# A Fourier convolution with a token-choice layer behind it: sums made in place and in other stages, and PSUM in two pools

## The chip, the cores and the metric

The kernel runs on one core of one Trainium2 chip. The metric is the device time of one execution in microseconds (us), lower is better.

## What is computed

The first part convolves every channel of `x` (8 batches, 6336 positions, 128 channels) with a filter `h` of the same length. The second part scores each position, picks the 128 best positions of each batch and adds a small gated two-layer network there.

```python
Xf = np.fft.rfft(x, n=2 * S, axis=1)
Hf = np.fft.rfft(h, n=2 * S, axis=0)
y = np.fft.irfft(Xf * Hf[None], n=2 * S, axis=1)[:, :S]
scores = np.einsum('bsd,d->bs', y, w_gate)
out = y.copy()
for b in range(B):
    top = np.argpartition(-scores[b], 128)[:128]
    ye = np.maximum(y[b, top] @ w1, 0) @ w2
    out[b, top] = y[b, top] + sigmoid(scores[b, top])[:, None] * ye
```

## The kernel before

The length 6336 is 99 x 64 (`N1` x `N2`), and the transform is done as matmuls in float32 over these two factors. Two batches at a time make a group, `g` = 0 to 3. The channels are taken in two halves of 64, `u` = 0 and 1. Each half of a group's `x` lies in one half of the tile `slots`, as eight blocks of 1024 columns, each with an upper part of 512 columns and a lower one. The stages of a group are generators, and `mix` (L481) interleaves them: at each step of its first argument it takes a given rate of steps of the others. The order of the instructions on each engine is this program order, since the schedule is manual (L40).

- **Stage A** (`stage_a`, L168) transforms over n1. For each block, `turn` (L158) makes on VectorE (DVE) the sum and the difference of the upper and the lower part, 114x512 each, into two tiles `xs` of the pool's tag "t", which has six buffers and also holds `tx` and `tm`. Eight blocks of two units: a unit is 16 matmuls into a tile of two PSUM banks, and one copy of 128x792 out of it, on ScalarE (ACT) or DVE. It turns at most three blocks ahead.
- **Stage b** (`stage_b`, L248, with `over_n2`, L228): 25 chunks of four frequencies. A chunk is 8 matmuls into the first bank of a tile `p`, two ACT operations that write the swapped and negated copy into its second bank (L234, L235), two DVE multiplications with the filter's spectrum (L239: into `slots`, and into `tx`), and an addition on GpSimd (POOL, L246). Tables `w` and spectra `hr` are loaded ahead on the SyncE queue (SP).
- **Stage c** (`stage_c`, L255): 16 units for each `u`, 16 matmuls into two banks and a copy of 99x1024.
- **Stage d** (`stage_d`, L265): 16 units of 8 matmuls, a copy, the store of the output and the scores (POOL multiplies, L287, DVE reduces, L289).
- **The choice** (`pick`, L292) of the group before runs beside all this as `side`, a chain on DVE with small matmuls: two searches of eight steps, then the places of the chosen rows (`lane`, written into `cmp`, L388 and L390), and a last matmul with them (L400). `feed` (L434) is the small network.

A group runs A for u=0, then b for u=0 with A for u=1 mixed in, then b for u=1 with c for u=0 (and `side`), then c for u=1 (with `side`), then d (with `side`). Group 0 has `stage_first` (L196), which also makes the filter's spectrum, in place of its first b. `stage_twice` (L222) copies half of that spectrum to a second place in memory; in group 0 it is mixed into c for u=1, and b for u=1 loads that half twice instead. The load of a group's second half of `x` starts when the d before it has ended, since its place is in use until then; the first half is loaded one stage earlier.

All PSUM tiles come from one pool of four tiles of two banks (L44), also those that use one bank.

Of the kernel before, what the change touches and what calls it, by code (L numbers as in the profile page):

```python
# [36 lines left out]
def conv_moe(ctx, tc, x, h, w_gate, w1, w2, fx_d, wb_d, wc_d, at_d, tri_d, cst_d, out):  # L37
# [6 lines left out]
    pp_ = ctx.enter_context(tc.tile_pool(name="pp_", bufs=4, space=PSUM))  # L44
# [5 lines left out]
    def bank():  # L50
        return banks()[:, 0:512]

    def psm():
        return pp_.tile([128, 1024], F32, tag="p", name="m")[:, 0:512]
# [56 lines left out]
    def ahead(key, only=None):  # L111
# [29 lines left out]
        while loaded[1] < len(spectra) and loaded[1] <= i + DEEP:  # L141
            item = spectra[loaded[1]]
            if item[1] != key[1]:
                break
            ht = hr[:, loaded[1] % 8 * 512:loaded[1] % 8 * 512 + 512].rearrange("p (t k d) -> p t k d", t=2, d=HD)
            loaded[1] += 1
            k0, kn = kchunks[item[3]]
            once = item[1:3] == (0, 1)
            for e in (slice(0, 64), slice(64, 128)) if once else (slice(0, 128),):
                nc.sync.dma_start(out=ht[e, :, 0:kn], in_=hd[0:64 if once else 128, item[2], item[3], :, 0:kn])  # L150
            have["h", item] = ht
# [4 lines left out]
    turned = {}  # L156

    def turn(d0):  # L158
# [9 lines left out]
    def stage_a(half, c0, lead=()):  # L168


        blocks = [(half, d) for d in range(0, HD, 8)]
        todo = blocks + list(lead)
        yv = yp[:, c0 // 2:(c0 + D) // 2].rearrange("p (b j) k t -> p b j t k", b=2)
        for i, d0 in enumerate(blocks):
            for d in todo[i:i + 3]:
# [20 lines left out]
    def stage_first():  # L196


        for ci, (k0, kn) in enumerate(kchunks):
# [19 lines left out]
            over_n2(0, k0, kn, wt, hv[:, 0])  # L219
            yield  # L220

    def stage_twice():  # L222

        for ci, (k0, kn) in enumerate(kchunks):
            nc.sync.dma_start(out=hd[64:128, 1, ci, :, 0:kn], in_=hd[0:64, 1, ci, :, 0:kn])
            yield

    def over_n2(c0, k0, kn, wt, ht, adds=nc.gpsimd):  # L228

        pt = banks()  # L230
        for j in range(kn):
            product(pt[:, j * D:(j + 1) * D], wt[:, j], row(k0 + j, c0, D))
        pv, pw = (pt[:, o:o + kn * D].rearrange("p (k b) -> p k b", b=D) for o in (0, 512))
# [4 lines left out]
        def times(dst, src, t):  # L238
            v.tensor_tensor(out=dst, in0=src.rearrange("p k (b j t) -> p k b j t", b=2, t=2),  # L239
# [8 lines left out]
    def stage_b(g, u, adds=(nc.gpsimd,)):  # L248
        for ci, (k0, kn) in enumerate(kchunks):
            key = ("b", g, u, ci)  # L250
            ahead(key)
            over_n2(u * D, k0, kn, have.pop(key), have.pop(("h", key)), adds[ci % len(adds)])
            yield

# [10 lines left out]
    def stage_d(g, ss):  # L265
# [3 lines left out]
        for m0 in range(0, N2, nd):  # L269
# [14 lines left out]
            for b in range(nb):  # L284
                tm = tp.tile([N1, nd, D], F32, tag="t", name="tm", bufs=6)
# [218 lines left out]
    rest(stage_a(0, D, [(1, 0), (1, 8)]))  # L504
# [3 lines left out]
    for i, _ in enumerate(stage_first()):  # L508
        if NK - 12 <= i < NK - 4:
            load(x[0, 1], 0, [i - NK + 12])  # L510
    ahead(("b", 0, 1, 0))
    side = iter(())
    twice = stage_twice()
    fed = []
    for g in range(G):
        last = g == G - 1
        c = stage_c(0, (1, 1, 0))
        if g:
            mix(stage_a(0, 0, [(1, 0), (1, 8)]), (side, 0.1))
            a = stage_a(1, D)  # L520
# [9 lines left out]
        mix(b, (c, 0.67 if g else 0.4), (side, 0.2))  # L530
# [9 lines left out]
        mix(stage_c(1, (1,)), (side, 0.9), (twice, 1.6))  # L540
# [9 lines left out]
        rest(twice)  # L550
# [96 lines left out]
```

## Time and profile before

| | |
|---|---|
| median of 3 runs | 1041.99 us (1041.69 to 1043.3) |
| the profiled execution, its own time | 1042.09 us |
| its span | 1040.3 us |
| TensorE (PE) busy | 909.1 us, 87% |
| DVE busy | 648.2 us, 62% |
| ACT busy | 554.5 us, 53% |
| POOL busy | 436.1 us, 42% |
| mean granted TensorE clock | 0.941 of 2.4 GHz |

The span runs from the first instruction to the last; the execution's own time is 1.8 us longer. PE is the busiest engine over the span, but the shares are means over stages that have different limits, so the stages have to be read one at a time. PE records come two to a float32 matmul: a unit of A or c is 32 records, a chunk of b 16.

### The profile page before, as it was taken

The page shows a single profiled execution, that of the slowest core. Times are in us where ns is not written, and L with a number is a line of the kernel's source. Part 1 is how long each engine was busy: PE and PEld are TensorE (multiplying, and loading weights), DVE is VectorE, ACT ScalarE, POOL GpSimd, SP SyncE. Part 2 cuts the span into 40 slices and gives each one's busy share as a digit, 9 for nine tenths or more (in the row PEclk, how much of TensorE's full clock was granted, in tenths as well). Part 3 has the DMA queues.
Part 4 walks back from the last instruction along what each step waited for, and adds up shares of the span by engine and source line. Part 5 has one row for each costly group of instructions (what it writes and reads, how often), then busy time and mean ns, then how long its engine had stood idle before and what let it go on. Part 6 is the DMA issues. An engine that isn't in the chain of part 4 may idle for free. (4 is left out here: it accounts for less than half of the span.)

```text
span 1040.3 us, 34561 instructions
## 1 busy us (share of the span) xinstructions
PE 909.1 (87%) x14707; PEld 798.9 (77%) x14707; DVE 648.2 (62%) x1250; ACT 554.5 (53%) x781; POOL 436.1 (42%) x340
## 2 busy tenths in 40 slices
PE   6899798899978899999688999999688999999565
PEld 5898797887676799877577899877577899877444
DVE  5466656304559867745868767735758777645773
ACT  4677576542357876523366776522466876432001
POOL 0045235317615755056425654057335763067101
PEclk9899899999969999999889999999889999999768
DMA  9289639856577887056847877055847882065100
GB/s 364 87 249 340 212 111 253 304 146 204 194 276 248 274 265 261 19 157 192 306 143 221 267 241 262 3 172 183 316 136 218 276 251 77 3 193 171 37 6 10
DMA packets 103545, 198.86 MB, mean 191 GB/s; under 512 B 11360, under 2 KB 28896, under 8 KB 103392
## 3 DMA queue, kind: packets, MB, share of 16 engines
q1 hardware_dynamic: 89504, 169.65, 50.0%
q10 hardware_dynamic: 13376, 25.96, 8.4%
q8 instruction: 116, 1.90, 0.7%
q0 software_dynamic: 512, 1.05, 0.3%
q14 instruction: 37, 0.30, 0.1%
HBM read 160.40 MB, written 39.45 MB: 192 GB/s over the span
## 5 line engine op out<-in xcount | busy, mean ns | idle before, releaser
L246 POOL TENSOR_TENSOR slots<-slots,tx 128x512 f32<-128x512 f32 (+1 forms) x200 | 259.4, 1312 | 316.4 <-DVE tx L239 273.5
L67 ACT COPY slots<-p 128x792 f32<-128x792 f32 (+3 forms) x266 | 248.3, 938 | 163.1 <-PE p L63 78.7
L63 PE MATMUL p<-wc,slots 128*64 128x128 f32 (+1 forms) x4096 | 246.2, 275 | 2.7 <-POOL slots L246 2.6
L287 POOL TENSOR_TENSOR tm<-hr,wg 99x512 f32<-99x512 f32 x120 | 158.8, 1344 | 210.5 <-issue 151.2
L63 PEld LDWEIGHTS p<-wc,slots 128*64 128x64 f32 (+1 forms) x4096 | 228.6, 127 | 4.9 <-POOL slots L246 3.7
L63 PE MATMUL p<-slots,w 128*64 128x128 f32 (+1 forms) x2900 | 201.7, 284 | 28.7 <-DMA w<-tab_wb 9.3
L63 PEld LDWEIGHTS p<-slots,w 128*64 128x64 f32 x2900 | 172.0, 139 | 42.2 <-ACT p L234 8.7
L289 DVE TENSOR_REDUCE sc<-tm 99x4 f32<-99x512 f32 x128 | 87.5, 686 | 154.7 <-POOL tm L287 154.4
L186 PE MATMUL p<-fx,xs 50*64 50x99 f32 x4608 | 142.3, 281 | 43.8 <-issue 20.5
L186 PEld LDWEIGHTS p<-fx,xs 50*64 50x64 f32 x4608 | 127.0, 157 | 59.4 <-issue 32.2
L239 DVE TENSOR_TENSOR slots<-p,hr 128x512 f32<-128x512 f32 (+1 forms) x175 | 119.2, 681 | 78.3 <-ACT p L235 76.0
L281 ACT COPY hr<-p 99x1024 f32<-99x1024 f32 x64 | 64.8, 1013 | 165.7 <-PE p L277 133.2
L234 ACT ACTIVATE p<-p 64x512 f32<-64x512 f32 (+1 forms) x200 | 113.1, 566 | 60.9 <-PE p L63 55.3
L277 PE MATMUL p<-slots,w 99*99 99x256 f32 x512 | 122.2, 379 | 3.9 <-ACT slots L67 3.9
L164 DVE TENSOR_TENSOR xs<-slots 114x512 f32<-114x512 f32 x144 | 104.7, 774 | 29.8 <-PE p L186 13.3
L277 PE MATMUL p<-slots,hr 99*99 99x256 f32 x512 | 121.1, 377 | 0.0
L239 DVE TENSOR_TENSOR tx<-p,hr 128x512 f32<-128x512 f32 (+1 forms) x175 | 118.1, 675 | 0.0
L235 ACT COPY p<-p 64x512 f32<-64x512 f32 (+1 forms) x200 | 110.8, 554 | 6.3
L277 PEld LDWEIGHTS p<-slots,w 99*99 99x99 f32 x512 | 82.2, 163 | 30.7 <-ACT slots L67 4.5
L277 PEld LDWEIGHTS p<-slots,hr 99*99 99x99 f32 x512 | 83.4, 163 | 27.5
L69 DVE COPY slots<-p 99x1024 f32<-99x1024 f32 (+2 forms) x54 | 48.7, 902 | 35.5 <-ACT slots L67 20.4
L63 PE MATMUL p<-slots 128*64 128x64 f32 (+1 forms) x664 | 46.6, 249 | 2.3 <-ACT p L234 2.3
(90 smaller groups left out, 509.2 us busy)
## 6 DMA issues: line engine op xcount, KB each, us to landing
w<-tab_wb SPq DMA_DIRECT2D x172, 256.0 KB
hr<-hd SPq DMA_DIRECT2D x144, 256.0 KB
slots<-in_x SPq DMA_DIRECT2D x64, 512.0 KB
out<-hr ACTq DMA_DIRECT2D x64, 396.0 KB
w<-tab_at SPq DMA_DIRECT2D x64, 153.1 KB
hr<-tab_at SPq DMA_DIRECT2D x64, 153.1 KB
hr<-hd SPq DMA_DIRECT2D x48, 128.0 KB
slots<-tab_wb SPq DMA_DIRECT2D x20, 256.0 KB
```

What stands on the lines that cost most here:

```text
L63: nc.tensor.matmul(out[a:b], table[:, a:b], moving, start=start, stop=stop)
L67: nc.scalar.copy(out=dst, in_=src)
L164: v.tensor_tensor(out=xt[0:HX].rearrange("p d n -> p (d n)"), in0=flat[0:HX, o:o + XB // 2], in1=flat[0:HX, o + XB // 2:o + XB], op=op)
L186: nc.tensor.matmul(pt[c * 64:(c + 1) * 64, o:o + N1], xt[c][e, q * 4 + j], fx[e, c * N1:(c + 1) * N1], start=True, stop=True)
L234: nc.scalar.mul(out=pw[0:64], in_=pv[64:128], mul=-1.0)
L235: nc.scalar.copy(out=pw[64:128], in_=pv[0:64])
L239: v.tensor_tensor(out=dst, in0=src.rearrange("p k (b j t) -> p k b j t", b=2, t=2), in1=ht[:, t, 0:kn].rearrange("p k (j t) -> p k j t", t ...
L246: adds.tensor_tensor(out=yv, in0=yv, in1=tx.rearrange("p k (j t) -> p k j t", t=2), op=ALU.add)
L277: nc.tensor.matmul(pt[:, i * 2 * D:(i + 1) * 2 * D], at[:, i % 2, c], zp[:, :, c * N2 + m], start=(c == 0), stop=(c == 1))
L281: nc.scalar.copy(out=yt.rearrange("p b n (u d) -> p (n u) b d", u=2), in_=pt.rearrange("p (n b d) -> p n b d", b=nb, d=HD))
L287: (v if b and m0 >= N2 - 2 * nd else nc.gpsimd).tensor_tensor(out=tm, in0=yt[:, b], in1=wg[0:N1].unsqueeze(1).broadcast_to([N1, nd, D]), o ...
L289: v.tensor_reduce(out=ss[:, b, m0:m0 + nd], in_=tm, axis=AX.X, op=ALU.add)
```

## The change

- `turn` needs no tiles: the sum goes into the lower part of the block before it (for the first block into a new tile `spare`), the difference in place of the upper part. The tag "t" has five buffers.
- All of a group's first half is turned before its stage A: four blocks in the second half of c for u=1, four in d (`fold`). In group 0, three blocks are turned in `stage_first`. The second half's first six blocks are turned in stage A of the first half.
- PSUM: a pool of two tiles of two banks (A, c, d, the first part of `stage_first`) and one of four single banks (b, the choice, the network). In `over_n2` the product and its swapped copy are two tiles, and the second multiplication and the addition are left for the next chunk's start (`end`).
- In A for u=1 of the later groups every second copy is on DVE (`share=2`), before one in eight.
- `stage_twice` is issued whole after `stage_first`, so that each spectrum is one load of 256 KB.
- `side` is no longer mixed into A; its rate in b for u=1 is 0.26, before 0.2; in d it runs through at 0.5.

```diff
-    pp_ = ctx.enter_context(tc.tile_pool(name="pp_", bufs=4, space=PSUM))
+    pp_ = ctx.enter_context(tc.tile_pool(name="pp_", bufs=2, space=PSUM))
+    ps_ = ctx.enter_context(tc.tile_pool(name="ps_", bufs=4, space=PSUM))
...
     def bank():
-        return banks()[:, 0:512]
+        return ps_.tile([128, 512], F32, tag="s", name="s")
...
-        turned[d0] = []
-        for op in (ALU.add, ALU.subtract):
-            xt = tp.tile([128, 8, N2], F32, tag="t", name="xs", bufs=6)
-            v.tensor_tensor(out=xt[0:HX].rearrange("p d n -> p (d n)"), in0=flat[0:HX, o:o + XB // 2],
-                            in1=flat[0:HX, o + XB // 2:o + XB], op=op)
-            turned[d0].append(xt)
+        above, below = (flat[0:HX, i:i + XB // 2] for i in (o, o + XB // 2))
+        sums = flat[:, o - XB // 2:o] if o else spare
+        v.tensor_tensor(out=sums[0:HX], in0=above, in1=below, op=ALU.add)
+        v.tensor_tensor(out=above, in0=above, in1=below, op=ALU.subtract)
+        turned[d0] = [t.rearrange("p (d n) -> p d n", n=N2) for t in (sums, flat[:, o:o + XB // 2])]
...
-                empty(i % 4 != 3 or not q, yv[:, :, j:j + 2], src.rearrange("p b (j t k) -> p b j t k", j=2, t=2))
+                empty((2 * i + q) % share != share - 1, yv[:, :, j:j + 2], src.rearrange("p b (j t k) -> p b j t k", j=2, t=2))
...
-        pt = banks()
+        pv, pw = (bank()[:, 0:kn * D] for _ in range(2))
...
         times(yv.rearrange("p k (b j) t -> p k b j t", b=2), pv, 0)
-        tx = tp.tile([128, KC, D], F32, tag="t", name="tx", bufs=6)[:, 0:kn]
-        times(tx.rearrange("p k (b j t) -> p k b j t", b=2, t=2), pw, 1)
-        adds.tensor_tensor(out=yv, in0=yv, in1=tx.rearrange("p k (j t) -> p k j t", t=2), op=ALU.add)
+        def end():
+            tx = tp.tile([128, KC, D], F32, tag="t", name="tx", bufs=5)[:, 0:kn]
+            times(tx.rearrange("p k (b j t) -> p k b j t", b=2, t=2), pw, 1)
+            nc.gpsimd.tensor_tensor(out=yv, in0=yv, in1=tx.rearrange("p k (j t) -> p k j t", t=2), op=ALU.add)
+        return end
...
-            mix(stage_a(0, 0, [(1, 0), (1, 8)]), (side, 0.1))
-            a = stage_a(1, D)
+            rest(stage_a(0, 0, [(1, d) for d in range(0, HD, 8)], 2))
+            a = stage_a(1, D, share=2)
...
-        mix(b, (c, 0.67 if g else 0.4), (side, 0.2))
+        mix(b, (c, 0.67 if g else 0.4), (side, 0.26))
...
-        mix(stage_c(1, (1,)), (side, 0.9), (twice, 1.6))
+        c = stage_c(1, (1,))
+        fold = iter(()) if last else turns(0)
+        mix(itertools.islice(c, 8), (side, 0.9))
+        mix(c, (side, 0.9), (fold, 0.5))
...
-        mix(itertools.islice(d, 13), (side, 0.5))
-        if not last:
-            turn((0, 0))
-            turn((0, 8))
-        mix(d, (side, 0.5))
+        mix(d, (side, 0.5), (fold, 0.3))
```

The order of DVE moves at three places that the prediction speaks of. In the rows, L164 and L165 of the change are the sum and the difference of a turn, L249 the two multiplications, L70 a copy out of PSUM; names before the arrow are what is written.

The first place is group 1's b for u=0 with A for u=1 mixed in, on DVE, some chunks after its start. Before:

```order
L164 TENSOR_TENSOR xs<-slots 114x512 x2
L239 TENSOR_TENSOR slots<-p,hr 128x4x64x2
L239 TENSOR_TENSOR tx<-p,hr 128x512
L239 TENSOR_TENSOR slots<-p,hr 128x4x64x2
L239 TENSOR_TENSOR tx<-p,hr 128x512
L239 TENSOR_TENSOR slots<-p,hr 128x4x64x2
L239 TENSOR_TENSOR tx<-p,hr 128x512
L164 TENSOR_TENSOR xs<-slots 114x512 x2
```

And in the change:

```order
L70 COPY slots<-p 128x2x2x2x99
L249 TENSOR_TENSOR tx<-s,hr 128x512
L249 TENSOR_TENSOR slots<-s,hr 128x4x64x2
L249 TENSOR_TENSOR tx<-s,hr 128x512
L249 TENSOR_TENSOR slots<-s,hr 128x4x64x2
L249 TENSOR_TENSOR tx<-s,hr 128x512
L249 TENSOR_TENSOR slots<-s,hr 128x4x64x2
L70 COPY slots<-p 128x2x2x2x99
```

The pair of turns between every three chunks is gone, and a copy stands in its place; a chunk's second multiplication (into `tx`) has moved behind that copy.

The second place is group 1's c for u=1 on DVE, two steps of the second search (`cmp`, `num` count, `ge` and `thr` take the next bound). Before:

```order
L317 TENSOR_TENSOR cmp<-rest,thr 99x384
L320 TENSOR_REDUCE num<-cmp 99x6
L324 TENSOR_SCALAR ge<-m 99x2x3
L327 TENSOR_REDUCE ge<-ge 99x2
L331 TENSOR_TENSOR thr<-ge,cst 99x6
```

And in the change:

```order
L335 TENSOR_TENSOR cmp<-rest,thr 99x384
L338 TENSOR_REDUCE num<-cmp 99x6
L164 TENSOR_TENSOR spare<-slots 114x512
L165 TENSOR_TENSOR slots<-slots 114x512
L342 TENSOR_SCALAR ge<-m 99x2x3
L345 TENSOR_REDUCE ge<-ge 99x2
L349 TENSOR_TENSOR thr<-ge,cst 99x6
```

A turn now stands between the count and the operation that reads the count's sum from PE (`m`), in four of the steps.

The third place is the end of group 1's d on DVE. Before:

```order
L289 TENSOR_REDUCE sc<-tm 99x4 x2
L164 TENSOR_TENSOR xs<-slots 114x512 x4
L289 TENSOR_REDUCE sc<-tm 99x4 x3
L287 TENSOR_TENSOR tm<-hr,wg 99x512
L289 TENSOR_REDUCE sc<-tm 99x4
L388 TENSOR_SCALAR cmp<-tri,last 99x128
L390 SCALAR_TENSOR_TENSOR cmp<-tri,first,cmp 99x128
```

And in the change:

```order
L307 TENSOR_REDUCE sc<-tm 99x4 x4
L406 TENSOR_SCALAR cmp<-tri,last 99x128
L408 SCALAR_TENSOR_TENSOR cmp<-tri,first,cmp 99x128
L406 TENSOR_SCALAR cmp<-tri,last 99x128
L408 SCALAR_TENSOR_TENSOR cmp<-tri,first,cmp 99x128
L164 TENSOR_TENSOR slots<-slots 114x512
L165 TENSOR_TENSOR slots<-slots 114x512
L307 TENSOR_REDUCE sc<-tm 99x4
L305 TENSOR_TENSOR tm<-hr,wg 99x512
```

The second batch's places (L388, L390, now L406, L408) have moved ahead of the last two units' scores, and one turn stands there in place of two.

## Rows read from the trace of the kernel before

**Rows 1.** By stretch: length, busy PE, PEld, DVE, ACT, POOL, clock, DMA share, GB/s.

```profile
111.00:142.00 31.00, 26.36 (x706) 24.58 (x708) 15.53 (x23) 17.79 (x21) 2.58 (x2) 0.89 0.33 97
142.00:193.00 51.00, 43.02 (x722) 40.17 (x717) 36.64 (x56) 35.74 (x57) 31.48 (x25) 1.00 0.90 245
...
280.00:304.00 24.00, 16.31 (x515) 15.23 (x514) 16.93 (x30) 13.57 (x15) 1.42 (x2) 0.76 0.87 318
304.00:359.00 55.00, 46.53 (x956) 40.15 (x957) 45.11 (x66) 42.21 (x68) 32.33 (x25) 0.92 0.76 238
359.00:443.00 84.00, 80.28 (x1402) 76.33 (x1402) 61.10 (x135) 55.67 (x74) 32.61 (x26) 1.00 0.57 188
...
527.00:591.00 64.00, 54.98 (x1098) 47.87 (x1100) 48.69 (x79) 45.78 (x78) 34.86 (x28) 0.92 0.68 210
...
760.00:823.00 63.00, 54.64 (x1086) 47.71 (x1084) 46.70 (x76) 45.06 (x76) 34.31 (x27) 0.92 0.68 209
```

**Rows 2.** Groups of instructions, shapes apart, 304 to 359 us: count, busy, mean ns, idle before.

```profile
L239 DVE TENSOR_TENSOR slots<-p,hr 128x512 f32<-128x512 f32 x25 | 17.1, 682 | 6.5 <-ACT p L235 6.5
...
L234 ACT ACTIVATE p<-p 64x512 f32<-64x512 f32 x26 | 14.8, 570 | 9.2 <-PE p L63 8.5
L235 ACT COPY p<-p 64x512 f32<-64x512 f32 x26 | 14.5, 558 | 0.8
```

**Rows 3.** Timeline of DVE in the same stage: start, length, instruction, idle before.

```profile
322.81 2.39 DVE L164 TENSOR_TENSOR xs<-slots 114x512 f32<-114x512 f32 x2 [0.28 <-POOL slots L246]
```

**Rows 4.** DVE groups, shapes apart, 280 to 303 us, the copy out of PSUM.

```profile
L69 DVE COPY slots<-p 128x792 f32<-128x792 f32 x2 | 2.0, 984 | 5.9 <-PE p L186 5.9
```

**Rows 5.** Timeline of PE in the same stretch, stage A of group 1.

```profile
280.04 2.97 PE L186 MATMUL p<-fx,xs 50*64 50x99 f32 x128
285.37 8.50 PE L186 MATMUL p<-fx,xs 50*64 50x99 f32 x219 [2.35 <-ACT slots L67]
294.66 2.96 PE L186 MATMUL p<-fx,xs 50*64 50x99 f32 x127 [0.79 <-issue]
300.88 1.92 PE L186 MATMUL p<-fx,xs 50*64 50x99 f32 x38 [3.26 <-issue]
```

**Rows 6.** DMA queues, 280 to 303 us: packets, MB, share.

```profile
q1 hardware_dynamic: 2736, 7.08, 83.8%
...
q8 instruction: 4, 0.07, 1.1%
```

**Rows 7.** Timeline of PE in group 0's A for u=0, with few transfers.

```profile
28.12 11.15 PE L186 MATMUL p<-fx,xs 50*64 50x99 f32 x381 [2.14 <-issue]
```

**Rows 8.** Timeline of DVE around the ends of group 1's and group 3's stage d.

```profile
495.11 2.49 DVE L164 TENSOR_TENSOR xs<-slots 114x512 f32<-114x512 f32 x4
...
965.09 1.33 DVE L390 SCALAR_TENSOR_TENSOR cmp<-tri,first,cmp 99x128 bf16<-99x128 f32 x1
```

**Rows 9.** Timeline of PE there.

```profile
498.32 1.89 PE L277 MATMUL p<-slots,hr 99*99 99x256 f32 x8
...
504.15 0.19 PE L400 MATMUL m<-lane,cmp 99*128 99x1 bf16 x1 [3.83 <-DVE cmp L390]
```

**Rows 10.** Timeline of DVE in group 1's c for u=1, one step of the search.

```profile
421.04 0.55 DVE L320 TENSOR_REDUCE num<-cmp 99x6 bf16<-99x384 bf16 x1
421.89 0.17 DVE L324 TENSOR_SCALAR ge<-m 99x6 f32<-99x6 f32 x1 [0.29 <-PE m L63]
```

**Rows 11.** Timeline of PE there.

```profile
421.69 1.95 PE L63 MATMUL p<-wc,slots 128*35 128x128 f32 x32
```

**Rows 12.** Timeline of PE at the start of group 0's A for its second half.

```profile
114.74 0.41 PE L186 MATMUL p<-fx,xs 50*64 50x99 f32 x4 [4.14 <-DVE xs L164]
116.06 7.07 PE L186 MATMUL p<-fx,xs 50*64 50x99 f32 x188 [0.90 <-DVE xs L164]
```

**Rows 13.** Waits, 142 to 193 us: total, times, longest.

```profile
PE p L63 <- DMA w<-tab_wb: 4.9, 8, 1.4
```

More of the change, by code (lines that the diff above doesn't have):

```diff
@@ L147, in ahead @@
             k0, kn = kchunks[item[3]]
-            once = item[1:3] == (0, 1)
-            for e in (slice(0, 64), slice(64, 128)) if once else (slice(0, 128),):
-                nc.sync.dma_start(out=ht[e, :, 0:kn], in_=hd[0:64 if once else 128, item[2], item[3], :, 0:kn])
+            nc.sync.dma_start(out=ht[:, :, 0:kn], in_=hd[:, item[2], item[3], :, 0:kn])
             have["h", item] = ht
     turned = {}
+    spare = cp.tile([128, XB // 2], F32, name="spare")
     def turn(d0):
@@ L160, in turn, with turns, stage_a @@
         o = half * XS + o // 8 * XB
-        turned[d0] = []
-        for op in (ALU.add, ALU.subtract):
-            xt = tp.tile([128, 8, N2], F32, tag="t", name="xs", bufs=6)
-            v.tensor_tensor(out=xt[0:HX].rearrange("p d n -> p (d n)"), in0=flat[0:HX, o:o + XB // 2],
-                            in1=flat[0:HX, o + XB // 2:o + XB], op=op)
-            turned[d0].append(xt)
-    def stage_a(half, c0, lead=()):
+        above, below = (flat[0:HX, i:i + XB // 2] for i in (o, o + XB // 2))
[3 more added lines that the diff above has]
+        turned[d0] = [t.rearrange("p (d n) -> p d n", n=N2) for t in (sums, flat[:, o:o + XB // 2])]
+    def turns(half):
+        for d in range(0, HD, 8):
+            turn((half, d))
+            yield
+    def stage_a(half, c0, lead=(), behind=0, share=8):
         blocks = [(half, d) for d in range(0, HD, 8)]
-        todo = blocks + list(lead)
+        todo = [[] for _ in blocks]
+        for i, d in enumerate(lead):
+            if i + behind < len(blocks):
+                todo[i + behind].append(d)
         yv = yp[:, c0 // 2:(c0 + D) // 2].rearrange("p (b j) k t -> p b j t k", b=2)
         for i, d0 in enumerate(blocks):
-            for d in todo[i:i + 3]:
+            for d in blocks[i:i + 3] + todo[i]:
                 if d not in turned:
@@ L196, in stage_first @@
     def stage_first():
+        end = None
         for ci, (k0, kn) in enumerate(kchunks):
@@ L218, in stage_first @@
                 nc.sync.dma_start(out=hd[0:128 - 64 * u, u, ci, :, 0:kn], in_=hv[0:128 - 64 * u, u, :, 0:kn])
-            over_n2(0, k0, kn, wt, hv[:, 0])
+            if end:
+                end()
+            end = over_n2(0, k0, kn, wt, hv[:, 0])
             yield
+        end()
     def stage_twice():
@@ L225, in stage_twice, with over_n2 @@
             nc.sync.dma_start(out=hd[64:128, 1, ci, :, 0:kn], in_=hd[0:64, 1, ci, :, 0:kn])
-            yield
-    def over_n2(c0, k0, kn, wt, ht, adds=nc.gpsimd):
-        pt = banks()
+    def over_n2(c0, k0, kn, wt, ht):
+        pv, pw = (bank()[:, 0:kn * D] for _ in range(2))
         for j in range(kn):
-            product(pt[:, j * D:(j + 1) * D], wt[:, j], row(k0 + j, c0, D))
-        pv, pw = (pt[:, o:o + kn * D].rearrange("p (k b) -> p k b", b=D) for o in (0, 512))
+            product(pv[:, j * D:(j + 1) * D], wt[:, j], row(k0 + j, c0, D))
         nc.scalar.mul(out=pw[0:64], in_=pv[64:128], mul=-1.0)
@@ L238, in times @@
         def times(dst, src, t):
-            v.tensor_tensor(out=dst, in0=src.rearrange("p k (b j t) -> p k b j t", b=2, t=2),
+            v.tensor_tensor(out=dst, in0=src.rearrange("p (k b j t) -> p k b j t", k=kn, b=2, t=2),
                             in1=ht[:, t, 0:kn].rearrange("p k (j t) -> p k j t", t=2).unsqueeze(2).broadcast_to(
@@ L243, in over_n2, with stage_b @@
         times(yv.rearrange("p k (b j) t -> p k b j t", b=2), pv, 0)
[L244 to L248 removed]
+        def end():
[3 more added lines that the diff above has]
+        return end
+    def stage_b(g, u):
+        end = None
         for ci, (k0, kn) in enumerate(kchunks):
@@ L251, in stage_b @@
             ahead(key)
-            over_n2(u * D, k0, kn, have.pop(key), have.pop(("h", key)), adds[ci % len(adds)])
+            if end:
+                end()
+            end = over_n2(u * D, k0, kn, have.pop(key), have.pop(("h", key)))
             yield
+        end()
     def stage_c(u, acts):
@@ L510, in conv_moe @@
             load(x[0, 1], 0, [i - NK + 12])
+        if i in (NK - 5, NK - 3, NK - 1):
+            turn((0, (i - NK + 5) * 4))
+    stage_twice()
     ahead(("b", 0, 1, 0))
     side = iter(())
-    twice = stage_twice()
     fed = []
```

8 lines of the change are left out of this document (4 added, 4 removed).

## The prediction, made before the changed kernel ran

> **What bounds the kernel now.** The share of busy time says PE, 87%, but I read the busy time stage by stage first [rows 1], and in each stage what ends last. Three kinds of stage come out. In group 1 from 359 to 443 us (b with c, then c alone) PE is busy 80.3 of 84 us: PE bounds it, and nothing that only frees another engine helps. In b with A for u=1 (304 to 359 us, and the same stage of groups 2 and 3, 64 and 63 us) PE is busy 46.5 of 55, 55.0 of 64 and 54.6 of 63 us: some 8.5 us each are PE's waits. And in stage A alone (280 to 304 us) PE is busy 16.3 of 24 us, at a granted clock of 0.76.
>
> In the second kind the groups and the timeline of DVE say why. DVE is busy 45.1 of 55 us, and the spectrum's multiplication takes 0.68 us [rows 1, 2]. A pair of turns there takes 2.39 us after a wait of 0.28 us [rows 3]: a turn needs a buffer that a POOL addition must give back, and one of its two runs beside such additions. Four turns at the end of d take 2.49 us together, 1.24 a pair [rows 8]. So on DVE three chunks and a pair of turns take 3 x 1.2 + 2.67 = 6.3 us (back to back the multiplications start every 0.6 us), and PE's three chunks and two units of A in that time need about 5.
>
> In the third kind the timeline of PE shows a run of 127 records that takes 2.96 us when it runs, and yet the next starts 6.2 us after it, at 300.88 [rows 5]. No engine released that wait. The page's instruction queue has 116 packets for 14707 matmuls and as many weight loads, 254 to a packet: one packet is 127 records, and four of them come in this stretch, beside 7.08 MB of loads [rows 6]. With few transfers 381 records, three packets, take 11.15 us, 3.7 each [rows 7]. So PE waits here for its own instructions behind the loads of `x` and the tables. **The Trainium skill**, page "Runtime: NRT & Kernel Launch", section "Instruction fetch mechanics", says that the next block is fetched while the current one runs and that crossing a boundary is mostly hidden. By this trace it isn't: 3.26 us are idle before 300.88 alone.
>
> **The parts and what they cost.** I work in the profiled execution's own time, 1042.1 us, 0.1 above the median of the runs.
>
> *b with A, groups 1 to 3.* Of six pairs of turns four leave for A, c and d: 4 x 2.39 = 9.6 us off DVE [rows 3]. Six more copies come to DVE at 0.98 us [rows 4]: 5.9 on, and off ACT. DVE falls from 45.1 to about 41.5 and no longer bounds; PE's busy time, 46.5, is the floor, a gain of 8.5 at most. I don't take all of it. A chunk's product may start when the first multiplication of the chunk two before is done, and that one waits for both ACT operations, 0.57 + 0.56 us, then takes 0.68 [rows 2]: 1.8, with handovers some 2.1 us, while PE has mostly a chunk and a unit, 1.85, to do meanwhile. Some 0.1 to 0.25 us of wait a chunk, 2.5 for the 25, remain: 55 becomes 49, **-6**. I take the same for groups 2 and 3, whose network steps have waits of their own: **-18** in all, between 0 (the waits move to the two-deep buffers) and -26 (PE's busy time is reached).
>
> Why does the first multiplication still wait, when product and copy are separate tiles? In the built order it still waits for ACT. The Trainium skill, page "PSUM — Partial Sum Buffer", section "PSUM bank collisions raise a hardware error", has it that two engines may not read one bank's same partitions at once, and ACT reads the product there. In the trace DVE waits for those copies 6.5 us in this stage [rows 2], which agrees. Without that rule the chain would be 1.1 us shorter and the stage would come down to its floor, -26 in place of -18.
>
> *Stage A of groups 1 to 3, and the end of d.* All sums are ready when A begins, so DVE isn't waited for (part of the 2.35 us before 285.37 [rows 5]). But the packets still come one in 6.2 us while the loads run, which begin with the end of d as before: A spans about four packets, so it stays near the 22 to 23 us of group 1. What goes is the wait at the end of d in groups 1 and 2: 3.83 us of PE on the last places [rows 9], because the turns stood ahead of them on DVE and slowed POOL [rows 8]. Now the choice is a step further by then (5 + 14 + 8 = 27 steps, before 1 + 4 + 14 + 7 = 26), and that step's DVE work has two units of d to finish. As the loads, and so the packets, start from d's end either way, I take 3 of each 3.83: **-6**, bounds -2 and -9. After group 3's d the same two pairs of operations (1.33 us the longest [rows 8], 2.2 together) leave the chain into the last choice: **-2**.
>
> *The turns that moved into c for u=1, groups 1 and 2.* Here the search sets the pace: its count ends, PE's small matmul follows, DVE goes on after 0.29 us idle [rows 10], and PE, whose unit takes 1.95 us [rows 11], waits for the next count every 2.04. A pair of turns now stands in that idle time and takes 1.24: each of 4 steps is 1.24 - 0.29 = 0.95 us longer, and PE's 1.95 cover only 0.1 of it. 8 x 0.95 = **+7.6**, between 0 and 9.9 (8 x 1.24). In group 0 there is no search and they are free; in d (POOL and PE have 1 us of slack a unit) and in A also, where PE waits for packets.
>
> *Group 0.* Its second A starts after 4.14 + 0.90 us of idle PE and then runs 188 records in 7.07 us, half speed [rows 12]; three blocks turned early end that. But the 25 copies of the spectrum now run in this stretch, whose DMA share was 0.33 [rows 1], and its 1414 records, counting the weight loads, are 5.6 packets: at 6.2 us each 34 us, where it took 31. Between -7.7 and +3.6 I take **-1**, near what the packets allow. The b after it waited 4.9 us for tables [rows 13] at a DMA share of 0.90 and 245 GB/s; single loads in place of halves make it like the later groups' b (0.57 from 359 on): **-3.5**, between 0 and -4.9.
>
> *Two-deep PSUM elsewhere.* c and A keep two tiles of two banks, b two chunks. A copy (1.0 to 1.1 us) fits well into a unit of c (1.95) and d. In b with c the ACT and DVE queues hold c's copies ahead of b's; no row shows the wait, so I bound it by 0 and 0.1 us for each of 100 chunks, +10, and take **+3**.
>
> Sum: -18 - 6 - 2 + 7.6 - 1 - 3.5 + 3 = -19.9, so **1022 us**.
>
> **Rivals.** (1) *Two-deep buffers take the gain.* If the queues on ACT and DVE lengthen a chunk's 2.1 us to over 3, PE waits about 1 us more on each, the stage with A stays at 55 and 64, and b with c, PE's best stage, loses 0.13 us for each of 100 chunks, +13. Then -6 - 2 + 7.6 - 1 - 3.5 + 13 = +8: 1050. For it: ACT is in order and has 42 of 55 us to do [rows 1]. Against: half of A's copies leave ACT, and single banks come free after the first multiplication. 0.11. (2) *The change only moves waits*: the stage with A gains 3 each, c loses all 9.9, group 0 nothing, the rings 5: 1042.1 - 9 - 6 - 2 + 9.9 + 5 = 1040; within 2 us of no change. 0.05, and 0.06 for values between this and the forecast's range. (3) *PE's floor is reached* in the stage with A: -26 and rings at 0, so 1011. 0.13. (4) *Packets are no bound*: if the wait in A was DVE's after all, a unit of A would take what its copy takes, about 0.95 us, 16 of them 15 in place of 22.7, 7.5 less three times: 1000. The page on instruction fetch named above would have it so; the runs of 127 records speak against it. 0.10.
>
> **How the numbers follow.** The forecast with its own range 1013 to 1034 has 0.55. A measurement can tell 0.2%, 2.1 us. Faster: 0.55 + 0.06 + 0.13 + 0.10 and a share of rival 2, 0.85; the same 0.04; slower 0.11. For 8 in 10 I leave out rival 1 and most of rival 4: 1004 to 1041.
>
> **What would show it.** Right: the stage of b with A at about 49 and 57 us with DVE no longer back to back; stage A still some 22 us with gaps at runs of 127 records; steps of about 3.0 us in the second half of c; no wait for places at d's end. Wrong: stage A at 16 us (rival 4); PE waits for the first multiplication or for copies of A all through b (rival 1); a longer second A in group 0, through the copies.

## The result and the profile after

The change takes 1027.05 us (median of 4 runs, 1024.21 to 1027.75), the kernel before 1041.84 us on the same chip: a ratio of 0.985, 95% interval 0.983 to 0.9875. The profiled execution is 1027.39 us, its span 1025.6; before it was 1042.09 and 1040.3. The forecast was 1022, with a range of 1004 to 1041. One profile further down, that of `places_later`, is of a disturbed execution (1048 us against a median of 1037), so I read from it only which instruction waits for which.

I cut both spans on PE where the records of one stage give way to those of the next (at the end of the start and ahead of d, at the last record of the stage before), in us:

| stretch | before | change | difference | forecast |
|---|---|---|---|---|
| start, A of `h` and of x0 | 44.3 | 47.6 | +3.3 | not placed |
| group 0, first stage to the end of c | 178.7 | 174.7 | -4.0 | -4.5 |
| d of group 0 | 57.0 | 57.0 | 0 | 0 |
| A for u=0, groups 1 to 3 | 68.4 | 69.1 | +0.7 | -6 with the next but two |
| b with A, groups 1 to 3 | 192.3 | 186.1 | -6.2 | -18 |
| b with c, then c, groups 1 to 3 | 238.9 | 241.1 | +2.2 | +7.6 and +3 |
| d of groups 1 and 2 | 126.0 | 116.6 | -9.4 | see A |
| from group 3's d on | 134.7 | 133.4 | -1.3 | -2 |
| span | 1040.3 | 1025.6 | -14.7 | -19.9 |

The total is near and the largest term isn't: b with A gave a third of what I wrote down. The busy time by stretch shows the same stages as [rows 1] (length, busy PE, PEld, DVE, ACT, POOL, clock, DMA share, GB/s):

```profile
111.00:141.00 30.00, 26.63 (x739) 22.98 (x736) 15.70 (x24) 19.87 (x26) 3.90 (x3) 1.00 0.71 202
141.00:193.00 52.00, 43.44 (x752) 41.71 (x750) 38.24 (x58) 35.88 (x57) 31.86 (x25) 1.00 0.86 273
279.30:303.50 24.20, 18.58 (x515) 15.91 (x514) 13.79 (x20) 13.50 (x15) 1.28 (x1) 0.78 0.84 315
303.50:359.00 55.50, 47.15 (x984) 38.88 (x986) 46.22 (x69) 39.32 (x66) 34.37 (x28) 0.97 0.81 257
359.00:441.00 82.00, 77.72 (x1376) 75.04 (x1373) 61.99 (x139) 52.95 (x69) 29.49 (x23) 1.00 0.54 178
521.70:587.00 65.30, 56.16 (x1112) 47.39 (x1114) 48.94 (x79) 42.13 (x74) 36.41 (x29) 0.95 0.72 222
748.50:813.00 64.50, 55.22 (x1116) 46.23 (x1118) 48.85 (x79) 42.05 (x74) 36.44 (x30) 0.97 0.73 225
```

From 303.5 on PE still has 8.35 us in which it isn't busy, and DVE is busy 46.2 of 55.5 us (this window reaches to the first unit of c and holds 29 chunks, that of [rows 2] 25). Over the same 29 chunks the kernel before took 58.3 us (304.0 to 362.3), in which PE wasn't busy for 9.7 and DVE was busy 48.4. So DVE lost only some 2 us of work, and its share stayed at 83%. What PE waits for there now (total, times, longest):

```profile
PE s L64 <- DVE slots L249: 7.9, 13, 1.3
PE s L64 <- DVE slots L70: 1.1, 1, 1.1
```

The groups of DVE and ACT in that stretch (count, busy, mean ns, idle before) answer to [rows 2, 4]:

```profile
L249 DVE TENSOR_TENSOR slots<-s,hr 128x512 f32<-128x512 f32 (+1 forms) x29 | 19.8, 684 | 9.3 <-ACT s L245 8.6
...
L70 DVE COPY slots<-p 128x792 f32<-128x792 f32 x8 | 7.8, 974 | 0.0
...
L244 ACT ACTIVATE s<-s 64x512 f32<-64x512 f32 (+1 forms) x29 | 16.4, 566 | 17.1 <-PE s L64 9.8 <-DVE tx L249 6.1 <-DVE slots L249 0.7
```

The last of these is new: ACT waits 6.1 us for a second multiplication (`tx`). The timeline (start, length, instruction, idle before) shows one such chain on DVE, ACT and PE:

```profile
329.25 1.47 DVE L164 TENSOR_TENSOR slots<-slots 114x512 f32<-114x512 f32 x1
330.75 0.69 DVE L165 TENSOR_TENSOR slots<-slots 114x512 f32<-114x512 f32 x1
331.36 0.68 DVE L249 TENSOR_TENSOR tx<-s,hr 128x512 f32<-128x512 f32 x1
331.96 0.68 DVE L249 TENSOR_TENSOR slots<-s,hr 128x512 f32<-128x512 f32 x1
...
332.14 0.57 ACT L244 ACTIVATE s<-s 64x512 f32<-64x512 f32 x1 [1.83 <-DVE tx L249]
...
330.45 0.91 PE L194 MATMUL p<-fx,slots 50*64 50x99 f32 x32
332.69 1.14 PE L64 MATMUL s<-slots,w 128*64 128x128 f32 x16 [1.33 <-DVE slots L249]
```

A turn stands on DVE from 329.25 to 331.44. Behind it stands the deferred `tx` of an earlier chunk. It holds one of the two banks for swapped copies, so ACT's next swap starts only at 332.14. PE has no third place for a product, and so it waits for the first multiplication of 331.96.

In group 0's b with c, 141 to 193 us, the same wait came where the table waits of [rows 13] had been. From the first to the last record of b the stage takes 46.0 us, before 47.3:

```profile
PE s L64 <- DVE slots L249: 6.2, 5, 1.4
```

The stretch just ahead of it, A for the second half mixed with c for u=0, grew. From the first unit of c to the first record of b it takes 21.9 us, before 18.9. Before, PE didn't wait at all there. Now A and c share two places, and PE waits for a copy ahead of every second unit of A (110 to 141 us):

```profile
PE p L194 <- ACT slots L68: 2.1, 5, 0.7
PE p L194 <- DVE slots L70: 0.5, 1, 0.5
```

Over the whole span the product of b now waits 37.1 us, before it was 28.7 (the page's groups):

```profile
L64 PE MATMUL s<-slots,w 128*64 128x128 f32 x2836 | 195.3, 283 | 37.1 <-DVE slots L249 26.8
```

At the end of d the wait of [rows 9] is gone. PE goes from the last unit to the places and on to A without a pause, since the places were done 0.1 us before:

```profile
497.82 0.35 DVE L408 SCALAR_TENSOR_TENSOR cmp<-tri,first,cmp 99x128 bf16<-99x128 f32 x1
...
496.56 1.89 PE L295 MATMUL p<-slots,hr 99*99 99x256 f32 x8
498.29 0.19 PE L418 MATMUL m<-lane,cmp 99*128 99x1 bf16 x2
```

And A for u=0 still runs by packets of 127 records, as in [rows 5]:

```profile
281.81 5.52 PE L194 MATMUL p<-fx,slots 50*64 50x99 f32 x175 [0.35 <-ACT slots L68]
289.17 5.81 PE L194 MATMUL p<-fx,slots 50*64 50x99 f32 x127 [1.84 <-issue]
295.73 4.50 PE L194 MATMUL p<-fx,slots 50*64 50x99 f32 x114 [0.76 <-issue]
```

### The profile page after: what moved, and what is told of

It reads as the page before. It is cut to its first block, busy times and chain, and to the rows that moved or that the text cites. A ratio compares the mean times of both kernels' runs of the same rounds, so it can differ in the third digit from the quotient of the medians.

```text
span 1025.6 us, 34445 instructions
## 1 busy us (share of the span) xinstructions
PE 905.7 (88%) x14707; PEld 785.6 (77%) x14707; DVE 678.4 (66%) x1268; ACT 539.3 (53%) x763; POOL 430.2 (42%) x340
## 5 line engine op out<-in xcount | busy, mean ns | idle before, releaser
L68 ACT COPY slots<-p 99x1024 f32<-99x1024 f32 (+2 forms) x248 | 231.7, 939 | 141.7 <-PE p L64 84.7
L64 PE MATMUL s<-slots,w 128*64 128x128 f32 x2836 | 195.3, 283 | 37.1 <-DVE slots L249 26.8
L64 PEld LDWEIGHTS s<-slots,w 128*64 128x64 f32 x2836 | 164.1, 137 | 54.1 <-DVE slots L249 37.2
L249 DVE TENSOR_TENSOR slots<-s,hr 128x512 f32<-128x512 f32 (+1 forms) x175 | 119.6, 683 | 81.6 <-ACT s L245 79.8
L194 PE MATMUL p<-fx,slots 50*64 50x99 f32 x4448 | 147.4, 273 | 22.2 <-issue 14.0
L244 ACT ACTIVATE s<-s 64x512 f32<-64x512 f32 (+1 forms) x200 | 113.1, 566 | 89.9 <-PE s L64 57.9
L194 PEld LDWEIGHTS p<-fx,slots 50*64 50x64 f32 x4448 | 121.8, 148 | 45.6 <-issue 25.9
L249 DVE TENSOR_TENSOR tx<-s,hr 128x512 f32<-128x512 f32 (+1 forms) x175 | 118.2, 676 | 0.0
L245 ACT COPY s<-s 64x512 f32<-64x512 f32 (+1 forms) x200 | 110.8, 554 | 6.3
L70 DVE COPY slots<-p 128x792 f32<-128x792 f32 (+2 forms) x72 | 66.3, 921 | 55.4 <-PE p L194 33.8
L165 DVE TENSOR_TENSOR slots<-slots 114x512 f32<-114x512 f32 x72 | 60.1, 834 | 2.5
L164 DVE TENSOR_TENSOR slots<-slots 114x512 f32<-114x512 f32 x67 | 50.3, 751 | 1.0
```

Source lines behind the costliest of these rows:

```text
L64: nc.tensor.matmul(out[a:b], table[:, a:b], moving, start=start, stop=stop)
L68: nc.scalar.copy(out=dst, in_=src)
L70: v.tensor_copy(out=dst, in_=src)
L244: nc.scalar.mul(out=pw[0:64], in_=pv[64:128], mul=-1.0)
L245: nc.scalar.copy(out=pw[64:128], in_=pv[0:64])
L249: v.tensor_tensor(out=dst, in0=src.rearrange("p (k b j t) -> p k b j t", k=kn, b=2, t=2), in1=ht[:, t, 0:kn].rearrange("p k (j t) -> p k j ...
```

## The experiments

My theory after this reading: the split of PSUM, with two places for a chunk, lengthens the chain DVE, ACT, DVE, PE, and takes back gains that the rest of the change makes. The rival: DVE's amount of work or PE's own time sets b with A, and PSUM doesn't matter. The runs were made in sets, each with its own runs of the kernel before (medians of 1037 to 1042 us), so kernels of different sets are compared by their ratios to it; 1% is 10.4 us.

### The PSUM split undone

`one_pool_deferred` gives the change one pool of four double tiles again; `one_pool_now` also issues the second multiplication and the addition at once, which is the kernel's old `over_n2`.

```diff
-    pp_ = ctx.enter_context(tc.tile_pool(name="pp_", bufs=2, space=PSUM))
-    ps_ = ctx.enter_context(tc.tile_pool(name="ps_", bufs=4, space=PSUM))
+    pp_ = ctx.enter_context(tc.tile_pool(name="pp_", bufs=4, space=PSUM))
...
-        pv, pw = (bank()[:, 0:kn * D] for _ in range(2))
+        pt = banks()
+        pv, pw = (pt[:, o:o + kn * D] for o in (0, 512))
```

> The changed kernel with its PSUM part alone undone: again one pool of four tiles of two banks, product and swapped copy in the two halves of one tile, second multiplication and addition at once. Theory 1 (the two-deep single banks, with copies and turns ahead of the first multiplication on DVE, are what keeps b with A at 56, 66 and 65 us): the four-deep tiles take these stages to about 51, 61 and 60 us, 5 less each, the start's A ends 3 us earlier (44.5 instead of 47.8), the five waits of 1.1 to 1.35 us in group 0's b go (-6): some 20 to 24 us less than the change, 1003 to 1007 us. Theory 2 (DVE's amount of work and PE's own time set b with A, PSUM does not matter): these stages stay within 1 us and the time is 1021 to 1027 us. Theory 3 (separate tiles were a gain, as the change has it): 1030 us or more.

> As the run with one pool, but the second multiplication and the addition stay deferred to the next chunk, so a chunk holds its tile of two banks longer. Theory 1: still four places, so most of the gain stays: 1004 to 1012 us; if the deferral itself costs, it shows here as 3 to 6 us against the run without it. Theory 2: 1021 to 1027 us, like the change.

`end_now` keeps the two pools and drops the deferral alone (`over_n2` calls `end()` itself):

> The change with its two PSUM pools, but the second multiplication and the addition of a chunk issued at once. Theory 1a (the deferral makes the swapped copy's bank free late: in the trace ACT's operation at L244 waits 1.83 us for a second multiplication that stands behind a turn, and PE then 1.33 us for the first multiplication): b with A gets 2 us shorter per group and group 0's b 3 us, 1015 to 1020 us. Theory 1b (two places per chunk are too few wherever the second multiplication stands): 1025 to 1029 us, the same. Theory 3 (the deferral hides something): slower, 1030 us and more.

Then the parts on the kernel before, alone: `before_deferred` has the deferral, `before_two_pools` the deferral and the split.

> The kernel before with one part of the change alone: the second multiplication and the addition of a chunk are left for the next chunk's start (one pool of four double tiles, turns and choice as before; the additions all on POOL as before). If the deferral is worth as much by itself as between the two runs with one pool (1018.0 and 1007.6 us): 10 us less than before, 1030 to 1033 us, 4 to 5 of it in the first stage of group 0. If it only works together with turns that need no tiles of tag t (a tile tx is held longer here, out of the same six): 1038 to 1045 us.

> The run before_deferred with PSUM split as in the change: two double and four single banks, product and swapped copy in separate tiles. If the split is a loss wherever it is made (two places for a chunk in place of up to four; the change against the same kernel with one pool: 1027 and 1007.6 us): 13 to 20 us more than before_deferred, 1043 to 1053 us, so slower than before. If it was a loss only beside the change's copies on DVE: within 4 us of before_deferred. If it is a gain here, 1025 us or less.

Measured, with the stretches of the profiled executions in us:

| kernel | median us | ratio to before, 95% | profiled, us | start | group 0 to end of c | b with A, 3 groups |
|---|---|---|---|---|---|---|
| before | 1037 to 1042 in five sets | 1 | 1042.1 | 44.3 | 178.7 | 192.3 |
| before_deferred | 1033.7 | 0.9948 (0.9918 to 0.9978) | 1040.6 | 45.5 | 176.8 | 189.3 |
| before_two_pools | 1056.1 | 1.0161 (1.0121 to 1.0202) | 1063.0 | 47.1 | 183.3 | 204.9 |
| one_pool_now | 1018.0 | 0.9805 (0.9768 to 0.9842) | 1026.7 | 45.2 | 173.3 | 184.1 |
| one_pool_deferred | 1007.6 | 0.9720 (0.9699 to 0.9741) | 1007.6 | 44.2 | 164.0 | 178.0 |
| end_now | 1033.4 | 0.9968 (0.9942 to 0.9994) | 1032.8 | 48.0 | 179.6 | 185.3 |
| the change | 1027.1 | 0.9852 (0.9830 to 0.9875) | 1027.4 | 47.6 | 174.7 | 186.1 |

The profiled executions of `before_deferred`, `before_two_pools` and `one_pool_now` took 7 to 9 us more than their medians, so their stretches are rather long.

The split is a loss wherever it is made. In three pairs that differ by it alone the intervals lie apart: 1.4% with the deferral (the change against `one_pool_deferred`), 1.7% without it (`end_now` against `one_pool_now`), and 2.1% on the kernel before, where it turns a gain of 0.5% into a loss of 1.6%. The rival, by which `one_pool_deferred` should have stayed at 1021 to 1027 us, falls: 0.9720 is 1012.7 us against the 1041.8 of the change's own set. In group 0's b with c the five waits of 1.1 to 1.4 us for the first multiplication are gone with one pool; of PE's waits in that stretch there remain

```profile
PE p L63 <- POOL slots L258: 2.1, 1, 2.1
PE p L63 <- DVE slots L69: 0.6, 1, 0.6
PE p L63 <- DMA w<-tab_wb: 0.4, 2, 0.2
```

In group 1's b with A they are gone too, but other waits take most of their place. The three longest there are

```profile
PE p L63 <- DVE slots L69: 2.8, 5, 1.2
PE p L63 <- DMA w<-tab_wb: 2.3, 3, 1.7
PE p L63 <- DVE tx L249: 1.8, 2, 1.1
```

PE isn't busy for 7.5 of 54.7 us, in the change for 8.35 of 55.8. So the 7.9 us of waits for the first multiplication aren't the price of the split in that stage: that is 1.1 us in group 1, and 4.0 and 3.0 in groups 2 and 3.

My own expectation failed twice. I put 5 us in each stage of b with A on the split, and `one_pool_now`, in its long execution, gained 2 in all three together; with the deferral the gain is 8.1 (186.1 to 178.0), and the split's larger price is in group 0, 10.7 us, and at the start, 3.4. And I suspected the deferral (theory 1a): the runs say that it is a gain in each of three pairs, 0.5% on the kernel before (half of the 10 us that I expected), 0.9% with one pool, 1.2% with two. Where it gains is seen: in group 0 above all, 4.9 us with two pools and 9.3 with one, of which the long execution of `one_pool_now` may hold a part. By which wait it does so I haven't settled.

### The copies given back to ACT

```diff
-            a = stage_a(1, D, share=2)
+            a = stage_a(1, D)
```

> The change with the copies of A for u=1 in groups 1 to 3 given back to ACT (one in eight on DVE, as before). Theory 1 (a copy of 0.98 us on DVE stands ahead of a multiplication that PE waits for): waits on DVE shrink, but ACT then has 6 copies more, 5.3 us, and A's two tiles come free later: within 2 us of 1027 us either way. Theory 2 (DVE's amount of work bounds the stage): DVE loses 6 x 0.98 = 5.9 us in each of three stages, which each get 3 to 5 us shorter, 1012 to 1018 us. If ACT becomes the bound: each stage 2 to 4 us longer, 1033 to 1039 us.

Measured: 1019.1 us, ratio 0.983 (0.9807 to 0.9854), which the interval doesn't part from the change. The profile shows where it acts: b with A takes 53.2, 64.1 and 64.1 us in place of 55.8, 65.7 and 64.6. So six copies off DVE, 5.9 us in each stage, gave 4.7 us over the three. The size is uncertain: in `folds_in_d`, `turns_late` and `no_second_half` below, where the copies stand as in the change, the three stages take 188.4, 187.6 and 184.1 us, here 181.5. DVE is busy only 40.3 us now in group 1's whole stage, 8.1 less than in the kernel before, and yet the waits behind the first multiplication stay, with two places as before:

```profile
PE s L64 <- DVE slots L249: 6.8, 13, 1.3
```

This is nearer to theory 1 than to theory 2. ACT's more work (44.15 of 53.2 us) didn't become a bound.

### The end of d: the choice's step or the turns

The kernel before had four `turn` operations (two pairs) and a late step of the choice at the end of d; the change moves both. Each was moved late again alone, though not quite to where it had stood. `places_later` has the second pair of places behind the scores of the last unit, by its trace: two units later than the change and one later than the kernel before, not where it stood, as the expectation has it:

```diff
-        mix(d, (side, 0.5), (fold, 0.3))
+        mix(itertools.islice(d, 13), (side, 0.5), (fold, 0.3)); mix(itertools.islice(d, 1), (fold, 1)); mix(d, (side, 0.5))
```

> The change with one thing put back: the step of the choice that makes the second pair of places in d comes one unit of d later, where it stood before, with all turns where the change has them. Theory A (the earlier step of the choice took away the 3.83 us wait at the end of d): d is 58.3 + 3.8 us again in groups 1 and 2, and the time 1033 to 1036 us. Theory B (the four turns ahead of the places, 2.49 us on DVE, made the wait): d stays at 58.3 to 58.8 us and the time within 1 us of the change. Both in part: the places end 2.5 us earlier than before but still after the last matmul, a wait of 1.3 us in each, 1030 us.

`turns_late` has the step of the change, and three pairs of turns (the kernel before had two) together behind the thirteenth unit:

```diff
-        mix(d, (side, 0.5), (fold, 0.3))
+        mix(itertools.islice(d, 13), (side, 0.5), (fold, 0.16)); mix(range(2), (fold, 1)); mix(itertools.islice(d, 1), (side, 1)); mix(d, (side, 0.5))
```

> The change with three pairs of turns of each d put together behind its thirteenth unit, where the kernel before had two pairs, and the second pair of places where the change has it. Theory A (it is the place of the choice's step that took away the wait at the end of d; the run with the later step had d at 64.1 us): d 58.3 to 59.5 us, the time within 3 us of the change. Theory B (turns ahead of the places make the wait): d 61 us or more in groups 1 and 2, 1032 us or more.

Measured: 1037.0 us (0.997, 0.9938 to 1.0001) and 1035.9 us (0.9965, 0.9937 to 0.9993). In `turns_late` d of groups 1 and 2 is 62.6 us each, in the change 58.3, before 63.0. PE waits for the places, in `places_later`

```profile
506.63 0.19 PE L418 MATMUL m<-lane,cmp 99*128 99x1 bf16 x1 [5.00 <-DVE cmp L408]
```

and in `turns_late`

```profile
500.40 0.18 PE L418 MATMUL m<-lane,cmp 99*128 99x1 bf16 x1 [3.43 <-DVE cmp L408]
```

So neither move alone takes the wait away: with the turns moved and the places last, or with the places early and three pairs of turns ahead of them, PE waits 5.00 and 3.43 us, where it is 3.83 in [rows 9]. What each move would be worth at the exact place of before isn't shown. In `turns_late` a turn also takes longer while POOL multiplies for the scores (DVE, then POOL; the second of the two DVE rows runs after POOL's end at 495.84):

```profile
494.64 1.75 DVE L164 TENSOR_TENSOR slots<-slots 114x512 f32<-114x512 f32 x1
496.43 0.69 DVE L165 TENSOR_TENSOR slots<-slots 114x512 f32<-114x512 f32 x1
...
494.57 1.27 POOL L305 TENSOR_TENSOR tm<-hr,wg 99x512 f32<-99x512 f32 x1 [0.51 <-ACT hr L299]
```

### The turns in c

```diff
-        mix(c, (side, 0.9), (fold, 0.5))
+        mix(c, (side, 0.9))
...
-        mix(d, (side, 0.5), (fold, 0.3))
+        mix(d, (side, 0.5), (fold, 0.6))
```

> The change with none of the turns in c for u=1: all eight of a group are made in d (rate 0.6), for groups 0 to 2. Theory of the prediction (a pair of turns between two counts of the search makes a step of c 0.95 us longer, and d has slack): the three waits of 1.0 us on the count in c of groups 1 and 2 go, c is 3 us shorter in each of them, d stays at 58.3 us, so 6 us less than the change, near 1021 us. Rival (d has no slack: its additions on POOL slow down beside turns, or the places at d's end come late again): c gains 3 each, d loses 3 or more in each of three groups: 1027 to 1033 us.

Measured: 1023.3 us, ratio 0.9844 (0.9811 to 0.9876), by the interval not apart from the change. In the profile b with c and c takes 79.1 us in both groups in place of 81.0, and d 58.5 in place of 58.3: the prediction's mechanism, 1.7 us a group of the 3 that I expected. In this execution b with A took 188.4 us, 2.3 more than in the change with no edit there, which hides most of it. In the change a turn stands behind the count, and each second step of c is 1.0 us longer (DVE, then PE; compare [rows 10, 11]):

```profile
433.44 0.68 DVE L164 TENSOR_TENSOR slots<-slots 114x512 f32<-114x512 f32 x1
434.15 0.69 DVE L165 TENSOR_TENSOR slots<-slots 114x512 f32<-114x512 f32 x1
434.76 0.16 DVE L342 TENSOR_SCALAR ge<-m 99x6 f32<-99x6 f32 x1
...
433.60 1.95 PE L64 MATMUL p<-wc,slots 128*64 128x128 f32 x32
436.55 0.18 PE L64 MATMUL m<-num,ones 99*64 99x6 bf16 x2 [1.01 <-DVE num L338]
```

### The packets of instructions

```diff
-            load(x[g + 1, 1], 1)
```

> The change without the load of the second half of x in groups 1 to 3: the channels of u=1 are computed there from what the slots still hold, and 4.2 MB per group less are moved while stage A for u=0 runs. Theory of the prediction (stage A for u=0 waits for packets of its own instructions behind these loads): the three stages of 24, 23 and 22 us fall to about 16, and the pauses at runs of 127 records shrink to under 1 us; 18 to 20 us less, 1007 to 1010 us. Rival (the copies out of two tiles, 0.95 us each, or a turn that waits for the load, set the stage): it stays at 20 us or more, 1018 to 1027 us.

Measured: 1014.6 us, ratio 0.9761 (0.9723 to 0.98). A for u=0 takes 17.8, 19.3 and 19.1 us in place of 24.1, 23.1 and 21.9, 12.9 us less in all; by the ratios the whole kernel gained 9.5. In the change PE's "issue" waits in these three stages are 3.1, 3.5 and 2.9 us, here 0, 0 and 0.8, and in group 1 runs are no more cut at 127. Most of the rest goes with the clock: 0.78 in group 1's A of the change, 1.00 here, with PE busy 18.7 and 14.7 us:

```profile
279.44 6.88 PE L194 MATMUL p<-fx,slots 50*64 50x99 f32 x224 [0.34 <-ACT slots L68]
286.47 3.92 PE L194 MATMUL p<-fx,slots 50*64 50x99 f32 x128 [0.15 <-DVE slots L70]
290.68 2.89 PE L194 MATMUL p<-fx,slots 50*64 50x99 f32 x96 [0.29 <-ACT slots L68]
```

What is left is mostly the copy: 16 units in 17.7 us, 1.1 each. The rival, 20 us or more, falls. The theory holds in kind; its 16 us was too low, and 18 to 20 us less in all too much. The Trainium skill, page "Runtime: NRT & Kernel Launch", section "Instruction fetch mechanics", has the crossing into a new block mostly hidden; the trace agrees without the load (148 GB/s in group 1's A) and not with it (315 GB/s).

### A version from all this, and one try too many

`one_pool_best` is `one_pool_deferred` with the copies on ACT and all turns in d.

> The one pool of four double tiles with deferred second multiplication (1007.6 us), the copies of A for u=1 back on ACT, and all turns in d. Theory (the three are independent: copies on ACT gave 2.6, 1.6 and 0.5 us in b with A under two pools, turns out of c 3 us twice): 997 to 1001 us. Rival (with four places DVE has no part in PE's waits, and ACT's six more copies come into the way): the copies give nothing or cost 2 us in each group, 1002 to 1010 us.

Measured: 1002.9 us (1001.6 to 1006.6), ratio 0.9638 (0.9606 to 0.9669), faster than both kernels. b with A takes 53.3, 60.9 and 59.7 us, 173.9 in all; the windows of the first two:

```profile
293.90:347.00 53.10, 46.57 (x984) 39.87 (x986) 41.04 (x63) 44.30 (x72) 34.64 (x28) 0.96 0.82 265
509.10:570.00 60.90, 54.12 (x1118) 47.03 (x1120) 43.76 (x74) 47.07 (x80) 37.87 (x31) 0.97 0.75 238
```

The median lies in the rival's range and not in the theory's 997 to 1001 us. By the ratios the gain over `one_pool_deferred` is 0.8%, 8.5 us, which is the theory's size; by the two medians, of different sets, it is 4.7. That the copies give nothing, as the rival has it, isn't so: b with A gave 4.1 us, and c 3.7, while the profiled execution (1006.6 us, the longest of five) had group 0 at 168.4 us in place of 164.0, which no edit explains.

`spread_load` is this version with six of the eight blocks of the second half of x loaded one at a time during A, on ACT's queue. The turns of that half come one block later, so one more pair of them falls into b with A:

```diff
-            load(x[g + 1, 1], 1)
+            load(x[g + 1, 1], 1, [0, 1])
...
+                if i < 12 and i % 2 == 0:
+                    load(x[g, 1], 1, [2 + i // 2], nc.scalar)
```

> The best version so far (1002.9 us), with the load of the second half of x spread over stage A for u=0: two of its eight blocks at the end of d as before, the other six one at a time on ACT's queue, each behind two copies of A. Theory (A's packets of instructions wait behind loads that are all queued at once; without that load A fell from 24, 23 and 22 to 17.8, 19.3 and 19.1 us): A for u=0 falls from 23.5 to 18 to 20 us in three groups, b with A, with one pair of turns more, grows by 0 to 1.5 us: 990 to 998 us. Rival (the packets wait for the bytes of the stage, however they are queued): A stays at 22 to 24 us, 1001 to 1006 us. Second rival (turns wait for the blocks, which now come later): A or b with A longer, over 1006 us.

Measured: 1012.4 us, ratio 0.9761 (0.9729 to 0.9794): slower than without the edit, a miss. A stays at 23.2, 25.2 and 24.8 us, and b with A takes 179.4 us in all, 5.4 more. In group 1's A PE no longer waits for "issue", but for a copy, and ACT for the store ahead of the loads that it issues (PE, then ACT):

```profile
280.87 7.88 PE L193 MATMUL p<-fx,slots 50*64 50x99 f32 x256 [4.89 <-ACT slots L67]
...
279.95 1.77 ACT L67 COPY slots<-p 128x792 f32<-128x792 f32 x2 [4.95 <-DMA out<-hr]
```

So in group 1 the loads on ACT's queue put a new wait into the engine that empties PSUM, by the profile for the landing of a store of d. In groups 2 and 3 PE still waits 4.8 and 2.0 us for "issue" in A, so there spreading the load didn't free the packets. Whether a spread load on another queue would free the packets wasn't tried.

## Why the prediction was right, and where it was not

- **b with A, -18: failed, -6.2.** The step that failed is "some 0.1 to 0.25 us of wait a chunk, 2.5 for the 25, remain": PE waited 7.9 us for first multiplications in group 1's stage. I had counted the handovers of one chunk (2.1 us) against PE's work of a chunk and a unit, but not what stands between them on DVE: a copy of 0.97 us, a turn of 2.2, and the deferred second multiplication, which I had moved to the next chunk without asking what its bank holds up. With one pool the stage gained 14.3 (192.3 to 178.0), and with the copies on ACT too 18.4 (to 173.9). So -18 is reached only without the split, which took 8.1, and without the copies on DVE, 4.1, which my sum counted on. The step before it, "DVE falls from 45.1 to about 41.5", failed too: over the whole stage DVE fell from 48.4 to 46.5 us, 1.9 and not 3.7. Four pairs of turns were worth 8.0 us and not 9.6, since the 2.39 of [rows 3] is one pair, and the twelve operations of the stage take 12.3. Nor would it have been enough: at 40.3 us of DVE, in `copies_on_act`, PE still waits 6.8 us.
- **The first multiplication waits for ACT: right.** DVE waits 8.6 us for L245 in that stage, and the rule of the Trainium skill, page "PSUM — Partial Sum Buffer", section "PSUM bank collisions raise a hardware error", that two engines may not access one bank's same partitions at once, agrees with that. Splitting the tile didn't shorten this chain, it only left two places for a chunk.
- **A for u=0 and the end of d, -6: right mechanism, -8.7.** A stayed at 22 to 24 us, held by packets behind the loads, as `no_second_half` shows. The end of d gave 4.7 in each of groups 1 and 2 and not 3. The prediction named both, the turns ahead of the places and the step, and neither alone took the wait away; its sum had taken 3 of 3.83 us, where more than the whole wait went.
- **After group 3's d, -2:** -1.3.
- **Turns in c, +7.6: the mechanism right (1.0 us a step, I wrote 0.95), the size too large.** Three steps in a group paid and not four, and without turns c was 79.1 us, 0.6 to 0.9 less than before: +2.2 in all. Two-deep PSUM cost nothing in b with c of groups 1 to 3, where I had put +3: with one pool (`one_pool_deferred`) b with c and c is 0.8 us longer in each.
- **Group 0, -4.5: -4.0, for other reasons.** From the end of the start's A to the first unit of c it gained 5.9 us where I had -1: the wait of 4.14 us and the slow run of [rows 12] are gone at a clock of 1.00 (in this execution; in `copies_on_act`, the same kernel up to there, the clock from the first record of A to the first unit of c was 0.68). From there to the end of c I expected -3.5 and it became 1.9 longer: b itself is 1.3 shorter, with as much idle PE as before (6.2 us, before 6.1), since the table waits went and the waits for two places came. A with c ahead of it is 3.0 longer; with one pool it is 18.9 us again. With one pool group 0 gains 14.7 (178.7 to 164.0), or 10.3 in `one_pool_best`.
- **The start:** +3.3, which I had not placed; the first record of the next stage comes at 47 to 49 us in all eight kernels with the split and at 44 to 45.5 in all six with one pool, so it is the two-deep PSUM; by which wait isn't settled.
- **Rivals.** Rival 1 was the one to weigh more: its mechanism took 14 us of what the change could have given (0.9720 against 0.9852), but in b with A, group 0 and the start, not in b with c of the later groups. Rival 2 had b with A nearly right (3 each, measured 2.1) and the rest wrong. Rivals 3 and 4 didn't come.

The forecast was 5 us too low: -18 was 12 too much, the start's 3.3 had no term, and group 0 and the end lacked 1.2; against that the turns in c cost 5.4 less, the +3 for b with c didn't come, and A with d gave 2.7 more. That the total came so near its forecast is luck in good part.

## What to carry to other kernels

When places in PSUM are split among more pools, count for each ring what can stand, on the engine that frees a place, between two of its uses: copies and long elementwise work included, since busy time below the span doesn't mean that the place comes free in time. A change of several parts can gain and still hold a part that loses; undo each part alone before judging the whole, which here was worth as much again as the change (0.9638 against 0.9852). Where two operations are both late at a stage's end, moving one alone may give nothing.

## What the runs showed of the hardware that I had not expected

PE's instruction packets wait behind data loads, by the "issue" waits between runs of 127 records: A of the same 512 records took 24.1 us at 315 GB/s, with 3.1 us of these waits and a clock of 0.78, and 17.8 us at 148 GB/s without one load of 4.2 MB, with none and a clock of 1.00. A DVE sum of 114x512 took 0.68 us alone and 1.75 us beside a POOL multiplication. In group 1, loads issued on ACT's queue went with an idle of 4.95 us on ACT that ended, by the profile, when an earlier store had landed.
